# Moving operand read in two alternating halves in the second matmul stage of a fused attention and gated MLP kernel

## The chip, the cores and the metric

The kernel runs on one core of a Trainium2 chip. The metric is the device time of one execution in microseconds (us). Lower is better.

## What is computed

Banded attention with 32 global tokens (8 batches, 8 heads, 512 local tokens, head dimension 64) makes 544 tokens of 512 features per batch. All 4352 tokens then go through a gated MLP without activation:

```python
attn_out = _attn_ref(q_l, k_l, v_l, q_g, k_g, v_g)     # (8, 8, 544, 64)
x = attn_out.transpose(0, 2, 1, 3).reshape(4352, 512)
a = x @ w1                                              # 512 -> 1024
b = x @ w2
h = a * b @ w3                                          # 1024 -> 1024
return h @ w_out                                        # 1024 -> 512
```

All tensors are float32.

## The kernel before

The kernel never forms h. Since nothing stands between w3 and w_out, it first multiplies the two matrices on the chip: `fold` (line 695) makes, for each of 8 blocks t of 128 rows, the 128x512 block t of w3 times w_out in PSUM, in float32. `fold_split` (lines 697 to 702) then splits each block into two tiles of type float32r, `w34h` (the value rounded to float32r, by a copy on ACT or DVE, `hi_of` at line 442) and `w34l` (the rest, by a subtraction on DVE, line 702). There are 8 tiles of each, 128x512, and they stay in SBUF (`W34`).

The tokens are worked on in 17 groups of 256 (two per batch, and one for the 8 x 32 global tokens). For each group there are four quarters, and each does this:

- `first` (lines 548 to 550): x times w1 and x times w2, for two blocks of 128 of the 1024 inner features. A product of two float32 matrices is made of three float32r matmuls (hi by hi, hi by lo, lo by hi); the moving operand is the token tile, 256 columns.
- `gate_a`, `gate_b`, `gate_hi`, `gate_lo`: the product a * b, split into `gh` and `gl` in the same way.
- `second` (lines 568 to 580): for each of the two blocks m and each 128 tokens t, three matmuls into the PSUM tile `acc`, which holds 128 tokens by 512 outputs. The stationary operand is a 128x128 piece of `gh` or `gl`; the moving operand is the whole of `w34h` or `w34l` of block m, 512 columns, read from the first to the last.

After the fourth quarter, `evict` (line 585) copies `acc` to SBUF and `store` writes it to DRAM in rows of 512.

So `second` issues 17 groups x 8 blocks x 2 token halves x 3 = 816 matmuls of 512 columns, and `first` 17 x 8 x 2 x 4 x 3 = 3264 of 256 columns.

The order of the work on each engine is written out by hand: the table `ORDER_OF` (lines 41 to 185) gives every step a place and, with the letters A, D and P, its engine where there is a choice. `add`, `take` and `read` declare what each step depends on, and `in_order` issues the steps by the table. Attention, the folding of the weights and the MLP are interleaved by it. The first matmul of `second` comes at about 108 us in the trace, after all of the folding.

Names used below: `w` is the PSUM tile of the folding, `w3f` and `wo` its operands, `acc` the PSUM tile of `second`, `ap` and `bp` those of `first`, `raw_w`, `raw_wo` and `raw_w12s` weights as they arrive in SBUF, of which each value is a pair of 32-bit words (so that `raw[:, :, 1]`, line 603, reads every other word), `x` the split token tiles, `xr` their source.

Of the kernel before, what the change touches and what calls it, by code (L numbers as in the profile page):

```python
# [14 lines left out]
def f(ap):  # L15
    return ap.bitcast(F32)
# [185 lines left out]
def band_attention_glu_kernel(  # L202
# [14 lines left out]
    nc = tc.nc  # L217
# [57 lines left out]
    T = {}  # L275
# [165 lines left out]
    def hi_of(dst, src, eng=None):  # L441
        (nc.scalar.copy if eng in (None, nc.scalar) else eng.tensor_copy)(dst, src)
# [94 lines left out]
    W12, W34 = {}, {}  # L537
# [30 lines left out]
    def second(key, w, m, ts=None):  # L568
        tw = min(w, 128)
        if m == 0:  # L570
            for t in range(0, w, 128):
                T["acc", key, t] = ps_acc.tile([128, 512], F32, tag="acc", name=f"acc{key[0]}_{key[1]}_{t}")
        wh, wl = W34[m]
        gh, gl = T["gh", m // 2 % 2], T["gl", m // 2 % 2]
        for t in range(0, w, 128) if ts is None else ts:
            sl = slice(t, t + tw)
            a = T["acc", key, t][0:tw]
            nc.tensor.matmul(a, gh[:, m % 2, sl], wh, start=(m == 0), stop=False)  # L578
            nc.tensor.matmul(a, gh[:, m % 2, sl], wl, start=False, stop=False)  # L579
            nc.tensor.matmul(a, gl[:, m % 2, sl], wh, start=False, stop=(m == 7))  # L580
# [116 lines left out]
    def fold_split(t, part, eng=None):  # L697
        if part == 0:
            W34[t] = tuple(const.tile([128, 512], F32R, tag=f"w34{e}{t}", name=f"w34{e}{t}") for e in "hl")
            hi_of(W34[t][0], T["w34", t], eng)  # L700
        else:
            nc.vector.tensor_sub(W34[t][1], T.pop(("w34", t)), f(W34[t][0]))

# [159 lines left out]
    def quarter(k, q):  # L865
# [27 lines left out]
        for ts in parts:  # L893
            for j in range(2):
                me = ("second", k, m + j, ts)
                deps = [("gl", n), ("w34l", m + j)]
                if m + j:
                    deps.append(("second", k, m + j - 1, None if j == 0 or not last else ts))
                if m + j == 0:
                    for e in range(0, w, 128):  # L900
                        take("acc", 2, ("acc", k, e), me)
                add(me, "PE", deps, second, key, w, m + j, ts)
                read(me, ("gh", n), ("gl", n), *[("acc", k, e) for e in range(0, w, 128)])
# [36 lines left out]
    def product(t):  # L940
        take(SUMS[t], 2 if SUMS[t] == "acc" else 1, ("w34", t), ("fold", t, 0))
        for j in range(8):
            add(("fold", t, j), "PE", [("unit", "w3", t, j // 4, 3), ("unit", "wo", j, 0, 3)] + [("fold", t, j - 1)] * (j > 0),
                fold, t, j)
            read(("fold", t, j), ("w34", t), ("w3f", t, j // 4))
        add(("w34h", t), "ACT DVE", [("fold", t, 7)], fold_split, t, 0)
        add(("w34l", t), "DVE", [("w34h", t)], fold_split, t, 1)
        read(("w34h", t), ("w34", t))
        read(("w34l", t), ("w34", t))
# [111 lines left out]
```

## Time and profile before

| | |
|---|---|
| median of the runs | 757.54 us |
| lowest run | 756.35 us |
| profiled execution, first to last instruction (span) | 754.5 us |
| TensorE matmul (PE) busy | 736.1 us, 98% of the span |
| VectorE (DVE) busy | 429.7 us, 57% |
| ScalarE (ACT) busy | 291.6 us, 39% |
| GpSimd (POOL) busy | 115.7 us, 15% |
| mean granted TensorE clock | 0.998 of full speed |

The profile shows the span of the profiled execution. What lies around it isn't in the trace; the median of the runs is 3.0 us above the span. In the profile, PE is the row of matmuls and PEld that of the loads of their stationary operands, which overlap them. The duration of a single matmul holds its way through the array, and the next one starts long before it has ended; so the cost of a matmul in a dense stretch is the distance from its start to the start of the next, its pace, and not its duration.

### The profile page before, as it was taken

To read this page: it belongs to the slowest core of one execution; us is meant where nothing else is said; L and a number is where in the kernel's file an instruction comes from. 1 tells how busy PE (TensorE), PEld (TensorE's weight loads), DVE (VectorE), ACT (ScalarE), POOL (GpSimd) and SP (SyncE) were. 2 spreads that over 40 slices of the span, in tenths; PEclk is the share of its full clock that TensorE was granted. 3 is DMA by queue.
4 is the path that set the end of the run, shared out by engine and by line. 5 is a ranking of instruction groups with operands and counts; after the bars stand their busy time and mean duration, and the time that the engine had idled before them with its cause. 6 is when DMAs were issued, how large, how long until landed. Compare 5 with 4: busy or idle time off the path is not lost.

```text
span 754.5 us, 24083 instructions
## 1 busy us (share of the span) xinstructions
PE 736.1 (98%) x10036; PEld 645.2 (86%) x10036; DVE 429.7 (57%) x1275; ACT 291.6 (39%) x853; POOL 115.7 (15%) x165
## 2 busy tenths in 40 slices
PE   3899999999999999999999999999999999999998
PEld 3355598988999998989999999899998999999997
DVE  2878888675565466555664557655566635432222
ACT  3777886555243333324234323244423242201010
POOL 2043564300020002130120001101020110000000
PEclk9999999999999999999999999999999999999999
DMA  7988578696586665587857396756675955520010
GB/s 238 311 285 252 167 222 244 192 264 165 157 220 168 188 194 153 167 193 197 220 165 202 106 248 189 214 139 174 167 197 168 254 151 135 134 69 15 1 43 29
DMA packets 96500, 131.98 MB, mean 175 GB/s; under 512 B 15592, under 2 KB 57704, under 8 KB 96392
## 3 DMA queue, kind: packets, MB, share of 16 engines
q1 hardware_dynamic: 96392, 130.45, 61.8%
q8 instruction: 79, 1.29, 0.8%
q14 instruction: 29, 0.24, 0.1%
HBM read 92.65 MB, written 37.75 MB: 173 GB/s over the span
## 4 chain that ended last, share of the span: by engine, by line
PE 97%; DMA 2%; SPq 0%; DVE 0%; issue 0%; ACT 0%
PE acc L578 9%; PE ap L548 9%; PE bp L548 9%; PE acc L580 8%; PE acc L579 8%; PE bp L549 8%; PE bp L550 8%; PE ap L549 8%; PE ap L550 8%; PE w L695 8%; PE s L350 4%; PE v L402 4%; PE sg L473 2%; PE gx L502 2%; DMA raw_wo<-in_wo_t_dram 1%; DMA vg<-in_vg_t_dram 1%
## 5 line engine op out<-in xcount | busy, mean ns | idle before, releaser
L548 PE MATMUL ap<-x,w12h 128*128 128x256 f32 x512 | 144.1, 281 | 0.0
L548 PE MATMUL bp<-x,w12h 128*128 128x256 f32 x512 | 144.0, 281 | 0.0
L549 PE MATMUL bp<-x,w12h 128*128 128x256 f32 x512 | 142.1, 277 | 0.0
L550 PE MATMUL bp<-x,w12l 128*128 128x256 f32 x512 | 142.0, 277 | 0.0
L549 PE MATMUL ap<-x,w12h 128*128 128x256 f32 x512 | 142.0, 277 | 0.0
L550 PE MATMUL ap<-x,w12l 128*128 128x256 f32 x512 | 141.9, 277 | 0.0
L362 ACT ACTIVATE P<-P,mn 128x128 f32<-128x128 f32 x256 | 100.4, 394 | 60.8 <-DVE mn L357 29.2
L548 PEld LDWEIGHTS bp<-x,w12h 128*128 128x128 f32 x512 | 96.1, 188 | 4.0 <-issue 1.6
L548 PEld LDWEIGHTS ap<-x,w12h 128*128 128x128 f32 x512 | 96.1, 188 | 3.7 <-issue 1.8
L549 PEld LDWEIGHTS bp<-x,w12h 128*128 128x128 f32 x512 | 96.3, 188 | 2.1 <-issue 0.2
L549 PEld LDWEIGHTS ap<-x,w12h 128*128 128x128 f32 x512 | 96.3, 188 | 1.4
L550 PEld LDWEIGHTS bp<-x,w12l 128*128 128x128 f32 x512 | 96.5, 188 | 0.0
L550 PEld LDWEIGHTS ap<-x,w12l 128*128 128x128 f32 x512 | 96.4, 188 | 0.0
L357 DVE CUSTOM_DVE_ANT_0 P<-s,cs 128x128 f32<-128x128 f32 x256 | 62.5, 281 | 34.9 <-PE s L350 31.4
L695 PE MATMUL w<-wo,w3f 128*128 128x512 f32 x128 | 60.7, 616 | 4.7 <-DVE w3f L609 4.7
L326 POOL COPY K<-K 128x480 f32<-128x480 f32 x24 | 15.8, 662 | 246.5 <-DMA K<-in_kp_t_dram 210.0
L695 PEld LDWEIGHTS w<-wo,w3f 128*128 128x128 f32 x128 | 23.5, 194 | 30.2 <-issue 22.3
L362 ACT ACTIVATION_READ_ACCUMULATOR P<-P,mn 128x1 f32 x256 | 48.3, 189 | 0.0
L316 POOL COPY V<-vg 32x1024 f32<-32x1024 f32 x26 | 27.1, 1049 | 80.7 <-PE gx L507 45.9
L370 DVE STREAM_TRANSPOSE P<-P 128x1024 f32<-128x1024 f32 x28 | 34.7, 1238 | 5.8 <-ACT P L362 5.6
L316 ACT COPY V<-vg 32x1024 f32<-32x1024 f32 x31 | 32.4, 1045 | 14.2 <-PE gx L507 13.5
L350 PE MATMUL s<-K,q 64*32 64x128 f32 x2048 | 37.3, 275 | 0.0
(786 smaller groups left out, 1372.3 us busy)
## 6 DMA issues: line engine op xcount, KB each, us to landing
Pd<-P SPq DMA_DIRECT2D x112, 128.0 KB, 3.0
Pt<-Pd SPq DMA_DIRECT2D x28, 512.0 KB, 4.2
raw_w<-in_w_t_dram SPq DMA_DIRECT2D x24, 512.0 KB, 6.0
V<-in_v_t_dram SPq DMA_DIRECT2D x56, 192.0 KB, 5.3
K<-in_kp_t_dram SPq DMA_DIRECT2D x36, 272.0 KB, 3.9
V<-in_v_t_dram SPq DMA_DIRECT2D x36, 256.0 KB, 5.0
out_dram<-o SPq DMA_DIRECT2D x34, 256.0 KB, 4.0
q<-in_q_t_dram SPq DMA_DIRECT2D x32, 256.0 KB, 4.6
```

The lines of the kernel that those rows point to most:

```text
L316: (nc.scalar.copy if eng is nc.scalar else eng.tensor_copy)(to, src)
L350: nc.tensor.matmul(block(st[:, h], x, 128 * g), q[64 * h : 64 * h + 64, c : c + 32], window(m, h, 4 * g + x), start=True, stop=True, skip_ ...
L357: nc.vector.tensor_tensor_reduce(T["P", m][:, :, h, g], chunks(T["s", m][:, h, 128 * g : 128 * g + 128]), chunks(masks[g]), -0.125, 3.0e38 ...
L362: nc.scalar.activation(P, P, AF.Exp, bias=T["mn", m][:, g, h : h + 1], scale=-1.0, accum_out=T["sm", m][:, g, h : h + 1])
L370: nc.vector.transpose(P, P)
L548: nc.tensor.matmul(d, wh[:, k, c, :], x[:, 0, 0:w], start=(k == m % 2 == 0), stop=False, skip_group_check=True)
L549: nc.tensor.matmul(d, wh[:, k, c, :], x[:, 1, 0:w], start=False, stop=False, skip_group_check=True)
L550: nc.tensor.matmul(d, wl[:, k, c, :], x[:, 0, 0:w], start=False, stop=(k == 3), skip_group_check=True)
L578: nc.tensor.matmul(a, gh[:, m % 2, sl], wh, start=(m == 0), stop=False)
L579: nc.tensor.matmul(a, gh[:, m % 2, sl], wl, start=False, stop=False)
L580: nc.tensor.matmul(a, gl[:, m % 2, sl], wh, start=False, stop=(m == 7))
L695: nc.tensor.matmul(T["w34", t], T["w3f", t, j // 4][:, j % 4], T["wo"][:, j], start=(j == 0), stop=(j == 7))
```

## The change

`fold_split` takes the columns of the product in PSUM in two passes: first the even columns 0, 2, ..., 510, which go to positions 0 to 255 of the tile, then the odd columns, which go to positions 256 to 511. It reads PSUM with a step of two elements (8 bytes) and writes SBUF in one run of 512.

`second` gives the matmul a view of the same tile that runs over the two halves in alternation: position 0, 256, 1, 257, and so on. In this order the columns are 0, 1, 2, 3, ... again, so `acc`, `evict` and `store` are as before. Two columns that follow each other in the stream are 256 elements (1024 bytes) apart in the partition, forward, and then 255 elements back.

```diff
@@ second
-        wh, wl = W34[m]
+        wh, wl = (w.rearrange("p (a c) -> p c a", a=2) for w in W34[m])
@@ fold_split
             W34[t] = tuple(const.tile([128, 512], F32R, tag=f"w34{e}{t}", name=f"w34{e}{t}") for e in "hl")
-            hi_of(W34[t][0], T["w34", t], eng)
+            hi_of(by_halves(W34[t][0]), in_pairs(T["w34", t]), eng)
         else:
-            nc.vector.tensor_sub(W34[t][1], T.pop(("w34", t)), f(W34[t][0]))
+            nc.vector.tensor_sub(by_halves(W34[t][1]), in_pairs(T.pop(("w34", t))), by_halves(f(W34[t][0])))
+
+    def by_halves(ap):
+        return ap.rearrange("p (a c) -> p a c", a=2)
+
+    def in_pairs(ap):
+        return ap.rearrange("p (c a) -> p a c", a=2)
```

No instruction is added, removed or moved: every engine issues the same instructions on the same tiles in the same order, and only the patterns by which the 816 matmuls and the 16 splits address them differ.

## Rows read from the trace of the kernel before

**Rows 1.** The page: span, busy time of each engine, granted TensorE clock.
```profile
span 754.5 us, 24083 instructions
...
PE 736.1 (98%) x10036; PEld 645.2 (86%) x10036; DVE 429.7 (57%) x1275; ACT 291.6 (39%) x853; POOL 115.7 (15%) x165
...
PEclk9999999999999999999999999999999999999999
```

**Rows 2.** Busy time by stretch, with granted clock, DMA share and GB/s last.
```profile
core 0: us, PE busy (x) PEld busy (x) DVE busy (x) ACT busy (x) POOL busy (x), PEclk, DMA share, GB/s
...
107.90:754.50 646.60, 643.13 (x8994) 589.81 (x8992) 350.93 (x1043) 214.06 (x668) 73.91 (x98) 1.00 0.60 163
```

**Rows 3.** All waits of PE: us in total, times, longest.
```profile
PE warm L863 <- POOL og L252: 10.3, 1, 10.3
PE w L695 <- DVE w3f L609: 4.7, 1, 4.7
```

**Rows 4.** The chain that ended last, shares of the span by line.
```profile
by line: PE acc L578 8.8%; PE ap L548 8.8%; PE bp L548 8.6%; PE acc L580 8.3%; PE acc L579 8.3%; PE bp L549 8.3%; PE bp L550 8.3%; PE ap L549 8.3%; PE ap L550 8.3%; PE w L695 7.7%; PE s L350 4.5%; PE v L402 4.3%; PE sg L473 1.8%; PE gx L502
```

**Rows 5.** Timeline of PE around 400 us: start, duration (us), instruction.
```profile
399.35 0.39 PE L580 MATMUL acc<-w34h,gl__5961 128*128 128x512 f32 x1
399.57 0.39 PE L578 MATMUL acc<-w34h,gh__5951 128*128 128x512 f32 x1
399.80 0.39 PE L579 MATMUL acc<-w34l,gh__5951 128*128 128x512 f32 x1
...
400.72 0.39 PE L580 MATMUL acc<-w34h,gl__5961 128*128 128x512 f32 x1
400.95 0.28 PE L548 MATMUL bp<-x,w12h 128*128 128x256 f32 x1
401.06 0.28 PE L549 MATMUL bp<-x,w12h 128*128 128x256 f32 x1
```

**Rows 6.** The page's group of the folding's matmuls: busy us, mean ns | idle before.
```profile
L695 PE MATMUL w<-wo,w3f 128*128 128x512 f32 x128 | 60.7, 616 | 4.7 <-DVE w3f L609 4.7
```

**Rows 7.** The chain from 60 to 82 us, pieces of folding: start, us, what.
```profile
65.70 4.49 PE w L695 x10
...
71.07 1.72 PE w L695 x4
```

**Rows 8.** DVE casts of line 442 by tile: duration ns min/median/max, starts, shapes.
```profile
L442 DVE CAST x<-xr x18: 229/283/294, 155.3 to 639.1; 128x256 fp32r<-128x256 f32 x18
...
L442 DVE CAST w34h<-w x2: 681/686/692, 45.9 to 47.2; 128x512 fp32r<-128x512 f32 x2
L442 DVE CAST w12h<-raw_w12s x2: 294/294/295, 98.0 to 128.5; 128x256 fp32r<-128x256 f32 x2
```

**Rows 9.** Tile w34h: the other splits, and the first matmuls of the second stage.
```profile
L702 DVE TENSOR_TENSOR w34l<-w,w34h x8: 675/684/692, 46.6 to 96.5; 128x512 fp32r<-128x512 f32 x8
L442 ACT CAST w34h<-w x6: 576/586/588, 52.3 to 95.9; 128x512 fp32r<-128x512 f32 x6
...
L578 PE MATMUL acc<-w34h,gh__1203 x4: 388/388/390, 107.9 to 109.9; 128*128 128x512 f32 x4
```

## The prediction

> **What bounds the kernel now.** I read the page first, for which engine is full: PE is busy 736.1 of 754.5 us, at full clock in every slice, while DVE stands at 57% and ACT at 39% [rows 1]. A mean over the span can hide a stage with another limit, so the second view is the busy time from the first matmul of the second stage to the end: PE is busy 643.13 of 646.60 us, at a granted clock of 1.00 [rows 2]. The 3.5 us that are left are the last copy and store. The third view, PE's waits, has two entries, 10.3 us for a cleared tile at the start and 4.7 us for folded weights, both long before 107.9 us [rows 3, 9]. So once the second stage runs, TensorE never waits, and no other engine has to be faster for it. Whatever a matmul of the second stage costs more or less goes into the end time in full, and no cover exists for it.
>
> The chain that ended last says how much of the span these matmuls hold: lines 578, 579 and 580 have 8.8 + 8.3 + 8.3 = 25.4% of 754.5 us, 191.6 us [rows 4]. The code issues 816 of them, so one holds 235 ns of the chain, handovers to other work included. In a dense stretch the timeline gives the pace itself: seven starts from 399.35 to 400.95 us, 1.60 us, 229 ns for 512 columns [rows 5]. The matmuls of 256 columns behind them start 0.11 us apart. The price goes with the columns, as for a stream that is fed one column after the other.
>
> **The change part by part.** The matmuls: none is added, removed or moved, and 816 read their moving operand in another order. Before, four neighbouring float32 columns are 16 bytes in a row; now every column lies 1 KB from the one before. No matmul in this trace reads its moving operand with a step between elements, so the cost has no row and I bound it from both sides.
>
> From below: the folding's matmuls, plain float32, go through the same array with the same tile of 128x512, and the trace has two records for each matmul of the code (128 records, 64 matmuls) [rows 6]. Four records take 1.72 us in a dense stretch, 430 ns each [rows 7]. If such a record stands for two passes over its 512 columns, a pass takes 215 ns, and that is the fastest pace that any stream of 512 columns shows here. The second stage needs 229 ns. Were the new order to free it of the difference, 14 ns x 816 = 11.4 us would go: 743.1 us of span.
>
> From above: the 430 ns record is also the nearest row for a stream that takes each column at half the rate: the same tile shape and element size, two column times per column fetched. And the 14 ns between 215 and 229 say that the float32r stream is already a little slower than the array could go, so what feeds it is close to being the limit. The columns 256 elements apart can no longer come out of one piece of memory that was fetched for its neighbour. If the feeding gave at least two columns per fetch before and gives one now, the pace is at least half: between 430 ns (the record) and 2 x 229 = 458 ns (its own pace doubled). I take the middle, 444 ns, since the first leaves out the 14 ns that this stream now pays and the second doubles them. The term is (444 - 229) x 816 = 175.4 us, with ends of 164.0 and 186.9 us. If each of four columns had come out of one fetch which already sets the pace, it would be 4 x 229 = 916 ns, far above; that end stands among the rivals.
>
> The Trainium skill states a rule that speaks against this change: in "Advanced Engine Details and Errata", section "SBUF Cachelines", SBUF has lines of 16 bytes, at least two hits on a line are needed to absorb the access time, and another line on each access is penalised. It gives no price for TensorE. No run shown so far bears it out or refutes it for a moving operand; by its two-hit limit a pattern with one hit would land at half pace, near the 444 ns above.
>
> The splits: 8 copies and 8 subtractions read PSUM with a step of 8 bytes instead of 4. They take 586 ns on ACT (6), 686 ns on DVE (2) and 684 ns on DVE (8) now [rows 8, 9]. The nearest row for a stepped read is from SBUF: DVE's casts of 128x256 take 294 ns from every other word and 283 ns from a source in runs [rows 8], 11 ns more. I take nothing. Doubled, the sum would be 6 x 0.586 + 2 x 0.686 + 8 x 0.684 = 10.4 us, spread from 46 to 97 us over two engines. That work stands beside PE's folding and attention. Of PE's waits none is for a split [rows 3]; if this cover were gone at every one, all 10.4 us would be on the path. A gain is excluded, since the elements are as many as before.
>
> The rest: gates, evictions, transfers and their order stay. PE's slower pace gives each of them more time between deadlines, and since PE waits for none of them after 107.9 us, that time buys nothing.
>
> The sum: 754.5 + 175.4 + 0 = 929.9 us of span. The median lies 3.0 us above the span of the profiled execution, so 933 us. For the later verdict: a measurement of this kernel can tell about 2%, 15 us, from no change, which is 18.6 ns for each of the 816 matmuls.
>
> **The rivals.** First, the order of the columns costs nothing: what feeds the stream fetches single columns, or runs far enough ahead to hold both lines. For it speaks that stepped reads on DVE cost 11 ns in 283 [rows 8]; against it, that DVE's step of 8 bytes leaves two columns in 16 bytes, and 1 KB leaves one, and that this engine streams fewer columns in the same time (128x256 in 283 ns, 512 in 229 ns on PE). The pace stays 229 ns and the time is 757 us, within 2%. It decides as long as the pace stays under 229 + 18.6 = 248 ns. This is the other side: not slower.
>
> In a sentence beside it: the Trainium skill's page "TensorE: Matmul & The Clock Gate", section "Back-to-back issue gap", gives a pace by the number of columns alone, whatever the pattern of the source, and so has the change at no cost; its own figure of 518 cycles for 512 columns at the full clock is an estimate of 216 ns, which this trace's 229 ns exceeds.
>
> Second, the alternation helps: if the 14 ns come from neighbouring columns colliding in one piece of memory, reading from two places in turn removes them, and the time is 757.5 - 11.4 = 746 us, 1.5% faster. It can't pass 2% unless a pass is faster than any row shows.
>
> Third, the fetch is the limit by more than a factor of two: four columns share one now, and the pace becomes up to 916 ns. The term is (916 - 229) x 816 = 560.6 us, the time 1318 us. Against it, a stream so short of fetches would hardly come within 14 ns of the two-pass record's rate.
>
> Fourth, a part of the cost is hidden by a small buffer ahead of the array: with a pace half way, (229 + 444) / 2 = 336 ns, 87 us more, 845 us.
>
> **How the numbers follow.** Half rate: 0.60, with its own range from 757.5 + 164.0 = 921 to 757.5 + 186.9 = 944, widened by the splits' 10.4 us to 955 and, for less than half rate's full price, down to 890. No cost: 0.20. Partly hidden, 775 to 890: 0.08. Above 955: 0.10. Helped by more than 2%: 0.02. The likeliest case gives 933 us. To leave out no more than 2 in 10, the range must reach to the case of no cost: from 755 to 955 it holds 0.60 + 0.08 + 0.20 = 0.88. Faster 0.02, same 0.20, slower 0.78.
>
> **What would show it.** In the profile after, the starts of L578, L579 and L580 in a dense stretch should stand about 444 ns apart, and those of L548 to L550 0.11 to 0.12 us apart as now; the chain should give the three lines some 40% of the span; PE should be busy all the way behind the first of them; the granted clock should stay at 1.00. The splits should stay at 586 and 684 ns. The prediction is wrong if the starts stay near 229 ns, or if the time comes out longer while they do, by a wait or a lower clock.

## The result and the profile after

The changed kernel takes 744.49 us (median of 4 runs, 744.0 to 746.68) against 756.94 us before (median of 4). One of the four runs before took 1741.61 us, and the ratio, 0.9846 with a 95% interval from 0.9828 to 0.9864, goes by the fast runs alone. The changed kernel is 1.5% faster: clear of no change, but within the 2% that the prediction counted as the same. The prediction was 933 us, slower by nearly a quarter.

The rows of the page that answer to [rows 1], of the changed kernel:

```profile
span 742.2 us, 24082 instructions
...
PE 724.9 (98%) x10036; PEld 645.6 (87%) x10036; DVE 429.2 (58%) x1275; ACT 292.0 (39%) x853; POOL 115.0 (15%) x165
...
PEclk9899999999999999999999999999999999999999
```

The span is 12.3 us shorter than before, and PE is busy 11.2 us less. The other engines work as long as they did. The stretch behind 107.9 us, as in [rows 2]:

```profile
107.90:742.20 634.30, 630.64 (x8991) 589.30 (x8989) 351.36 (x1040) 214.47 (x668) 73.81 (x98) 1.00 0.60 166
```

It is 634.30 us long instead of 646.60, also 12.3 us less. The first matmul of the second stage starts at 107.4 us here, 0.5 us earlier than before, so 11.8 us of the gain lie behind it, where PE is as full as before and the granted clock is 1.00. The waits of PE, as in [rows 3]:

```profile
PE warm L869 <- POOL og L252: 9.0, 1, 9.0
PE w L695 <- DVE w3f L609: 4.7, 1, 4.7
PE v L402 <- DVE raw_w12s L605: 0.2, 1, 0.2
```

The two long ones lie ahead of the second stage, as before, and no wait for a gate, a split or an output tile has come in. The timeline of PE in a dense stretch of the second stage, as in [rows 5] (the rows left out are matmuls of the same three lines):

```profile
401.86 0.38 PE L579 MATMUL acc<-w34l,gh__6050 128*128 128x512 f32 x1
...
403.37 0.38 PE L580 MATMUL acc<-w34h,gl__6097 128*128 128x512 f32 x1
```

From the first row to the second are seven distances, 1.51 us, 216 ns each. Before it was 229 ns. Over the whole trace, the distances from each of the 816 to the next matmul add up to 191.1 us before and 179.8 us now: 11.3 us less, 14 ns each. The rest is the 0.5 us from before the stage and some tenths in the first stage (382.0 to 381.3 us); the spans of thirteen executions of the kernel before differ by more than that, from 752.2 to 757.0 us. The two tiles' splits:

```profile
L702 DVE TENSOR_TENSOR w34l<-w,w34h x8: 676/682/692, 46.4 to 96.1; 128x512 fp32r<-128x512 f32 x8
L442 ACT CAST w34h<-w x6: 586/587/590, 52.1 to 95.4; 128x512 fp32r<-128x512 f32 x6
```

The medians are 682 and 587 ns against 684 and 586 [rows 9]: reading PSUM by every other column costs nothing that these rows show.

### The profile page after: what moved, and what is told of

Its sections match the earlier page's. It is cut to its first block, busy times and chain, and to the rows that moved or that the text cites. A ratio compares the mean times of both kernels' runs of the same rounds, so it can differ in the third digit from the quotient of the medians.

```text
span 742.2 us, 24082 instructions
## 1 busy us (share of the span) xinstructions
PE 724.9 (98%) x10036; PEld 645.6 (87%) x10036; DVE 429.2 (58%) x1275; ACT 292.0 (39%) x853; POOL 115.0 (15%) x165
## 4 chain that ended last, share of the span: by engine, by line
PE 90%; DMA 6%; DVE 1%; POOL 1%; issue 1%; ACT 0%; SPq 0%; DVEq 0%; POOLq 0%
PE ap L548 8%; PE acc L578 8%; PE bp L548 8%; PE ap L549 8%; PE ap L550 8%; PE bp L550 8%; PE bp L549 8%; PE acc L580 8%; PE acc L579 8%; PE w L695 5%; PE v L402 4%; PE s L350 4%; DMA raw_wo<-in_wo_t_dram 3%; PE sg L473 2%; PE gx L502 2%; DMA raw_w12s<-in_w_t_dram 1%
## 5 line engine op out<-in xcount | busy, mean ns | idle before, releaser
L548 PE MATMUL ap<-x,w12h 128*128 128x256 f32 x512 | 143.9, 281 | 0.0
L548 PE MATMUL bp<-x,w12h 128*128 128x256 f32 x512 | 143.8, 281 | 0.0
L549 PE MATMUL ap<-x,w12h 128*128 128x256 f32 x512 | 141.9, 277 | 0.0
L549 PE MATMUL bp<-x,w12h 128*128 128x256 f32 x512 | 141.8, 277 | 0.0
L550 PE MATMUL ap<-x,w12l 128*128 128x256 f32 x512 | 141.8, 277 | 0.0
L550 PE MATMUL bp<-x,w12l 128*128 128x256 f32 x512 | 141.8, 277 | 0.0
L548 PEld LDWEIGHTS bp<-x,w12h 128*128 128x128 f32 x512 | 96.3, 188 | 3.3 <-issue 1.6
L548 PEld LDWEIGHTS ap<-x,w12h 128*128 128x128 f32 x512 | 96.3, 188 | 3.2 <-issue 1.8
L549 PEld LDWEIGHTS bp<-x,w12h 128*128 128x128 f32 x512 | 96.2, 188 | 1.4 <-issue 0.2
L549 PEld LDWEIGHTS ap<-x,w12h 128*128 128x128 f32 x512 | 96.2, 188 | 0.9
L550 PEld LDWEIGHTS bp<-x,w12l 128*128 128x128 f32 x512 | 96.2, 188 | 0.0
L550 PEld LDWEIGHTS ap<-x,w12l 128*128 128x128 f32 x512 | 96.1, 188 | 0.0
```

The lines of the kernel that those rows point to most:

```text
L548: nc.tensor.matmul(d, wh[:, k, c, :], x[:, 0, 0:w], start=(k == m % 2 == 0), stop=False, skip_group_check=True)
L549: nc.tensor.matmul(d, wh[:, k, c, :], x[:, 1, 0:w], start=False, stop=False, skip_group_check=True)
L550: nc.tensor.matmul(d, wl[:, k, c, :], x[:, 0, 0:w], start=False, stop=(k == 3), skip_group_check=True)
```

## The experiments

In all of them the number to read is the distance between starts in the second stage, from two rows of PE's timeline that are seven distances apart; only the moving read of `second` differs from the kernel named, unless something else is said. A time without a ratio beside it is that of one run.

**The order alone.** The splits of the changed kernel, with the read of before:

```diff
-        wh, wl = (w.rearrange("p (a c) -> p c a", a=2) for w in W34[m])
+        wh, wl = W34[m]
```

> The splits write the two halves as in the changed kernel, but the second stage reads the tile in one run of 512; so the 512 output columns come out with the even ones first and the odd ones behind. Theory A (the order of the moving read sets the pace): the starts of L578 to L580 go back to 226 to 232 ns apart, the span to 754.5 us, ratio to before 1.00. Theory B (the splits, or the values' new places in SBUF, bring the gain): the starts stay 216 ns apart and the span near 742 us, ratio 0.985.

```profile
408.56 0.40 PE L579 MATMUL acc<-w34l,gh__6050 128*128 128x512 f32 x1
...
410.18 0.39 PE L580 MATMUL acc<-w34h,gl__6097 128*128 128x512 f32 x1
```

1.62 us / 7 = 231 ns, a span of 755.2 us, and a ratio of 1.0003 (0.9989 to 1.0018). The splits bring nothing and cost nothing. The read's order is the whole effect.

**Three orders that tell why.** On the kernel before:

```diff
-        wh, wl = W34[m]
+        wh, wl = (w.rearrange("p (g a c) -> p g c a", a=2, c=4) for w in W34[m])
```

> The splits are those of before; the second stage reads each group of 8 columns as 0, 4, 1, 5, 2, 6, 3, 7, so that the stream alternates between two neighbouring pieces of 16 bytes; the output columns come out in that order. Theory 1 (two places far apart are needed, the neighbour collides): 226 to 232 ns between starts, span 754 us. Theory 2 (a run of neighbouring columns is what costs, any break of it frees the pace): 216 ns, span 742 us. Theory 3 (one column for each fetch of 16 bytes halves the rate once the fetch can't be kept): 430 ns or more, span 920 us.

```profile
402.93 0.38 PE L579 MATMUL acc<-w34l,gh__6050 128*128 128x512 f32 x1
...
404.44 0.38 PE L580 MATMUL acc<-w34h,gl__6097 128*128 128x512 f32 x1
```

216 ns and 746.46 us, as in the change, with two places only 16 bytes apart: the distance isn't what matters. Theory 1 falls.

```diff
-        wh, wl = W34[m]
+        wh, wl = (w.rearrange("p (c a) -> p a c", a=2) for w in W34[m])
```

> The splits are those of before; the second stage reads columns 0, 2, 4, ..., 510 and then 1, 3, ..., 511, a step of 8 bytes with no alternation; the output columns come out in that order. Theory 1 (two places far apart in turn are needed): 226 ns or more between starts, span 754 us or more. Theory 2 (any break of the run frees the pace): 216 ns, span 742 us. Theory 3 (fetches of 16 bytes): two columns for each fetch, no worse than 229 ns.

```profile
426.90 0.64 PE L579 MATMUL acc<-w34l,gh__5334 128*128 128x512 f32 x1
...
430.08 0.64 PE L580 MATMUL acc<-w34h,gl__5348 128*128 128x512 f32 x1
```

3.18 us / 7 = 454 ns, and 938.39 us in the one run: half rate by a step of 8 bytes, which neither of the two theories left had. Theory 2 falls: a break of the run isn't enough.

```diff
-        wh, wl = W34[m]
+        wh, wl = (w.rearrange("p (c a) -> p a c", a=4) for w in W34[m])
```

> The splits are those of before; the second stage reads columns 0, 4, 8, ..., then 1, 5, 9, ... and so on, a step of 16 bytes with no alternation; the output columns come out in that order. Theory 1 (two places far apart in turn are needed): 226 ns or more between starts, span 754 us or more. Theory 2 (any break of the run frees the pace): 216 ns, span 742 us. Theory 3 (one column for each fetch of 16 bytes halves the rate): 430 ns or more, span 920 us.

```profile
400.67 0.64 PE L579 MATMUL acc<-w34l,gh__4942 128*128 128x512 f32 x1
...
403.90 0.64 PE L580 MATMUL acc<-w34h,gl__4983 128*128 128x512 f32 x1
```

461 ns and 943.55 us. This is the half rate of theory 3 and of the prediction. It exists, with nearly the predicted time, but the change doesn't call it up. And theory 3 alone can't say why a step of 8 bytes, with two columns in each 16 bytes, costs as much as one of 16.

**Two new theories.** P: the memory gives pairs of columns. L: the stream is read in two lanes, of which one takes its even places and the other its odd places. They part where two places are read in turn, with a step of two in each:

```diff
-        wh, wl = W34[m]
+        wh, wl = (w.rearrange("p (a c b) -> p b c a", a=2, b=2) for w in W34[m])
```

> The splits are those of before; the second stage reads 0, 256, 2, 258, ..., 254, 510 and then 1, 257, 3, 259, ...: two places in turn as in the change, but in each place a step of two columns; the output columns come out in that order. Theory P (the memory gives two neighbouring columns, 8 bytes, per fetch, and the fetch is kept for at least one other one; half rate whenever the second column of a pair is not asked for soon): about 450 to 460 ns between starts, span 937 us, as with a step of two alone. Theory L (the stream is read in two lanes, its even and its odd places, and a lane goes at full rate as long as its own step is 8 bytes or less): 216 to 232 ns, span 742 to 755 us.

```profile
408.33 0.40 PE L579 MATMUL acc<-w34l,gh__6050 128*128 128x512 f32 x1
...
409.94 0.39 PE L580 MATMUL acc<-w34h,gl__6097 128*128 128x512 f32 x1
```

1.61 us / 7 = 230 ns, 756.78 us: the run's own time. Under L it has to be so, since a run too gives each lane a step of two columns. P falls, which wanted 450 ns.

The next two change places more often:

```diff
-        wh, wl = W34[m]
+        wh, wl = (w.rearrange("p (a c) -> p c a", a=4) for w in W34[m])
```

> The splits are those of before; the second stage reads 0, 128, 256, 384, 1, 129, ...: four places in turn; the output columns come out in that order. Theory P with room for two fetches only: the second column of a pair comes three fetches later and has to be fetched again, 450 to 460 ns, span 937 us. Theory P with room for four or more: 216 ns, span 742 us. Theory L: each lane jumps by 1 KB at each step, 450 ns or more.

```profile
413.72 0.44 PE L579 MATMUL acc<-w34l,gh__5951 128*128 128x512 f32 x1
...
415.67 0.45 PE L580 MATMUL acc<-w34h,gl__5961 128*128 128x512 f32 x1
```

```diff
-        wh, wl = W34[m]
+        wh, wl = (w.rearrange("p (a c b) -> p c a b", a=2, b=2) for w in W34[m])
```

> The splits are those of before; the second stage reads 0, 1, 256, 257, 2, 3, 258, 259, ...: two places in turn, but a pair of neighbours from each; the output columns come out in that order. If the 10 to 16 ns that the run loses come from one pair following the next out of the same place: 216 ns between starts, span 742 us. If they come from the two columns of one pair being asked for one right behind the other: 226 to 232 ns, span 754.5 us. Theory L: lanes of 0, 256, 2, 258 and 1, 257, 3, 259, at half rate or at full rate as in the run of two places with a step.

```profile
404.13 0.50 PE L579 MATMUL acc<-w34l,gh__5445 128*128 128x512 f32 x1
...
406.41 0.50 PE L580 MATMUL acc<-w34h,gl__5451 128*128 128x512 f32 x1
```

279 ns and 326 ns in these rows, 793.87 and 846.29 us; over all starts in the second stage the medians are 280 and 340 ns. In both orders each lane jumps between two places at every step. L expected half rate for the first and left half rate open for the second, and neither is as bad. That a lane keeps something of the place it left would fit; these runs don't show it.

**How much of a piece a lane uses.** If a lane fetches 16 bytes at a time, the number of its columns in a piece should count, and not its step. An order in which each lane takes two neighbours from each piece:

```diff
-        wh, wl = W34[m]
+        wh, wl = (w.rearrange("p (g a c) -> p g c a", a=2, c=2) for w in W34[m])
```

> The splits are those of before; the second stage reads each four columns as 0, 2, 1, 3; the output columns come out in that order. The stream's even places then ask for columns 0, 1, 4, 5, 8, 9, ..., its odd places for 2, 3, 6, 7, ...: each lane uses two columns of a piece of 16 bytes, neighbours, before it goes on to the next. Theory L16 (each lane fetches 16 bytes at a time, and a fetch that serves two columns falls slightly short of the array): 226 to 232 ns between starts, span 755 us, as the run and as two places with a step. Theory L4 (what a lane needs is a step of one column, whatever the piece): 216 ns, span 742 us.

```profile
407.31 0.40 PE L579 MATMUL acc<-w34l,gh__6050 128*128 128x512 f32 x1
...
408.93 0.39 PE L580 MATMUL acc<-w34h,gl__6097 128*128 128x512 f32 x1
```

231 ns, 756.0 us: theory L16. All orders by what a lane finds in each piece of 16 bytes before it goes on:

| order of the stream | columns per piece and lane | distance |
|---|---|---|
| 0, 256, 1, 257 (the change); 0, 4, 1, 5 | 4 | 216 ns |
| the run; 0, 256, 2, 258; 0, 2, 1, 3 | 2 | 229 to 231 ns |
| 0, 2, 4, 6; 0, 4, 8, 12 | 1 | 454, 461 ns |
| 0, 128, 256, 384, 1; 0, 1, 256, 257, 2 | 4 and 2, but each lane changes pieces at every column | 280, 340 ns (medians of all starts) |

**A rival for the run's loss: the loads.** While a matmul streams, the stationary operand of the next is loaded from SBUF too (PEld is busy 645.2 us beside PE's 736.1 in the 754.5 us of [rows 1]). To see whether the two get in each other's way, the load behind L578 is halved, in the kernel before:

```diff
-            nc.tensor.matmul(a, gh[:, m % 2, sl], wl, start=False, stop=False)
+            nc.tensor.matmul(a[0:64], gh[:, m % 2, t : t + 64], wl, start=False, stop=False)
```

> The kernel before, but the matmuls of line 579 use 64 of 128 columns of the stationary operand, so the hi by lo product is left out for half of the tokens; all moving reads are runs of 512. The load of 64 columns goes on while L578 streams. If the run's loss comes from the load reading SBUF beside it: the distance from L578 to L579 falls from 226 towards 220 ns, and the others stay. If it comes from the moving read alone: it stays at 226 ns, the span at 755 us.

```profile
408.68 0.39 PE L578 MATMUL acc<-w34h,gh__6050 128*128 128x512 f32 x1
408.91 0.39 PE L579 MATMUL acc<-w34l,gh__6050 128*64 128x512 f32 x1
...
409.36 0.39 PE L578 MATMUL acc<-w34h,gh__6050 128*128 128x512 f32 x1
409.59 0.39 PE L579 MATMUL acc<-w34l,gh__6050 128*64 128x512 f32 x1
```

The distance from L578 to L579 is 0.23 us in both pairs, and over all starts in the trace its median is 227 ns, the same as before, though the load for L579 now takes 134 ns instead of 188. The distance from L579 to L580 stays at 229 ns too. The time is 756.84 us. So the loss doesn't depend on the width of the load that goes on beside the read.

**Both stages.** If a run loses, the first stage loses too, with 3264 matmuls. On the changed kernel, the first stage's token tiles are read in alternation, and the stores put the rows in their places:

```diff
@@ first
-            x = X[key[0], k, key[1]]
-            nc.tensor.matmul(d, wh[:, k, c, :], x[:, 0, 0:w], start=(k == m % 2 == 0), stop=False, skip_group_check=True)
...
+            xh, xl = (X[key[0], k, key[1]][:, e, 0:w].rearrange("p (a c) -> p c a", a=2) for e in range(2))
+            nc.tensor.matmul(d, wh[:, k, c, :], xh, start=(k == m % 2 == 0), stop=False, skip_group_check=True)
...
@@ store
-            r = key[0] * S + 32 + 256 * key[1] + t
-            nc.sync.dma_start(out[r : r + 128], o)
+            r = key[0] * S + 32 + 256 * key[1]
+            nc.sync.dma_start(out[r : r + 256].rearrange("(a c) d -> c a d", a=2)[t // 2 : t // 2 + 64], o)
...
+            to = out.rearrange("(a e b s) c -> e b s a c", a=2, e=2, b=2)[t // 128]
+            for x in range(2):
+                nc.sync.dma_start(to[x, 0:32], o[64 * x : 64 * x + 64])
```

> The changed kernel, and the first stage too reads its token tiles in alternation (0, 128, 1, 129, ...), so that the rows of the gate tiles and of the output tiles stand for the tokens in that order; the stores write them to their places. If a run loses in the first stage what it lost in the second (dense starts now 113 to 122 ns apart, the mean of lines 548 to 550 at 116.8 ns): 108 to 110 ns between dense starts, some 5 ns x 3264 = 16 us less than the changed kernel, about 728 us, ratio to before 0.962. If 256 columns are bound by something else, such as the loads of the stationary operand, the starts stay at 113 ns or more: 744 us, ratio 0.984. If the stores by alternating rows delay the output tiles, PE shows waits on o and the time is above 744 us.

Two rows of the first stage in this kernel, fifteen distances apart:

```profile
402.01 0.28 PE L548 MATMUL ap<-x,w12h 128*128 128x256 f32 x1
...
403.69 0.28 PE L548 MATMUL ap<-x,w12h 128*128 128x256 f32 x1
```

1.68 us / 15 = 112 ns. The time is 735.93 us (median), a ratio of 0.9726 (0.9691 to 0.9762) to before: this version beats both kernels. The gain over the changed kernel is about 9 us, not the 16 expected: over all starts in the first stage the median goes from 114 to 112 ns and not to 108 to 110, and the distances add up to 371.7 us instead of 381.3. PE shows no wait on the output tiles.

The same edit on the kernel before, with the second stage in runs:

> The kernel before, with the alternation in the first stage alone (token tiles read as 0, 128, 1, 129, ..., stores to match); the second stage reads in runs. If the gains of the stages are independent: 111 to 112 ns between dense starts in the first stage, 226 to 232 ns in the second, some 9 us less than before, 748 us, ratio 0.988. If the second stage's loss depends on what the first left in place, its starts move from 226 to 232 ns.

```profile
402.73 0.40 PE L579 MATMUL acc<-w34l,gh__6050 128*128 128x512 f32 x1
...
404.34 0.39 PE L580 MATMUL acc<-w34h,gl__6097 128*128 128x512 f32 x1
```

747.93 us, a ratio of 0.9896 (0.9880 to 0.9913), with 230 ns in the second stage. Over all starts one of its distances did move as the second theory had it: from L578 to L579 the median is 234 ns instead of 227, and the 816 add up to 192.4 us instead of 191.1; why is open. The two gains add up within the interval: 0.9846 x 0.9896 = 0.974, and both together measured 0.9726.

Last, what holds the first stage at 112 ns, in the version with both stages:

```diff
-            nc.tensor.matmul(d, wh[:, k, c, :], xl, start=False, stop=False, skip_group_check=True)
+            nc.tensor.matmul(d[0:64], wh[:, k, c, 0:64], xl, start=False, stop=False, skip_group_check=True)
```

> The kernel with both stages in alternation, but the matmuls of line 549 use 64 of 128 columns of the stationary operand, so the hi by lo product of the first stage is left out for half of the inner features. The load of 64 columns goes on while L548 streams. If what keeps the first stage at 111 to 112 ns for 256 columns, against 216 / 2 = 108 ns by the second, is the load of the next stationary operand: the distance from L548 to L549 falls to 108 to 109 ns, the others stay at 111 to 112 ns, the time falls by some 3 ns x 1088 = 3 us. If it is the stream itself or a fixed price of each matmul: all stay at 111 to 112 ns.

```profile
400.01 0.28 PE L548 MATMUL ap<-x,w12h 128*128 128x256 f32 x1
...
401.67 0.28 PE L548 MATMUL ap<-x,w12h 128*128 128x256 f32 x1
```

Fifteen distances take 1.66 us instead of 1.68. Over all starts in the trace, one distance of three falls, by 3 ns from 112 to 109. But it is the distance from L549 to L550, not the expected one from L548 to L549, though the load for L549 takes 138 ns instead of 192. The one run takes 733.86 us, 0.6 us below the lowest of the four with both stages (734.45 to 738.47 us), so the time alone shows no gain. The matmul of half the width is thus followed 3 ns sooner; since it also writes half the output rows, the run doesn't say whether the stationary operand or the output has a part in the 112 ns. A kernel that reads the stationary operands of the first stage in alternation too gave no result, so no run shows what that would do.

## Why the prediction was wrong

- **What bounds the kernel** held. PE was full behind 107.9 us and still is, no other engine gave or took time, and what the matmuls saved went into the end in full: 11.3 us of distances, 12.3 us of span.
- **The splits at nothing** held, by their own rows (682 and 587 ns) and by the run that has them alone (1.0003).
- **The step that failed** is "If the feeding gave at least two columns per fetch before and gives one now, the pace is at least half". The words "gives one now" took the stream for a single reader that forgets a piece as soon as it asks for another. A reader of single columns in turn would have done to the alternation what happened to the steps of two and four. What the runs show in its place is that the even and the odd places of the stream count apart: with the change each of the two keeps to its own half, and finds four columns in a piece of 16 bytes where the run gave it two. Two readers, one for each, are the model for this and no more. The term was put at +175.4 us and measured -11.3 us.
- **The price of half rate** was nearly right and applied to the wrong order: the prediction put it between 430 and 458 ns and took 444, and steps of two and four columns measure 454 and 461 ns, at 938 and 944 us.
- **The lower bound** of 215 ns, from the folding's records read as two passes, was the answer: 216 ns. Whether such a record is two passes, no run shows, so the agreement may hold some luck. The sign was in the prediction's own rows, in the 14 ns between 215 and 229. They were read as a feed close to its limit, which fits the runs, since the order alone moves the pace, and then as a reason that this order must hurt. They were also the most that any order here won.
- **The second rival** named 746 us and got 744.5, and its price (11.4 us) is what the 816 matmuls gave (11.3). Its reason, neighbours that collide in one piece of memory, is only half right: two places 1 KB apart lose as much as the run when each lane uses two columns of a piece (230 ns). It had no share of its own in the chances within 2%, and the case within 2% was told as "no cost". The first rival's bound, a distance under 248 ns, held, but not its cause.
- The 518 cycles for 512 columns of the Trainium skill ("TensorE: Matmul & The Clock Gate", section "Back-to-back issue gap"), which the prediction took for an estimate of 216 ns, agree with the changed kernel's 216 ns; before the change the trace was 13 ns above it. The section calls this the gap of an isolated matmul, which the prediction left out, and gives about 131 ns for 512 columns in a sustained stream of loads and matmuls. The sustained streams here differ: none is faster than 216 ns.

## What to carry to other kernels

When a dense float32r stream's distance between starts lies above what the columns need, look at what the even and the odd places of the moving operand ask for: an order that gives each of them four neighbouring columns, such as two halves in alternation, took 229 ns to 216 ns here, and a median of 114 ns to one of 112 ns in the stage of 256 columns. The data can be laid out for it where it is written anyway, by the splits or the stores. A plain step of two or of four columns costs double here, so a layout that saves a copy by a stepped moving read should be priced at that.

## What the runs showed of the hardware that was not expected

A moving read of float32r in a plain run isn't the fastest one: 229 to 231 ns against 216 ns for 512 columns. A step of 8 bytes halves the rate (454 ns) and one of 16 bytes hardly adds to it (461 ns), while an alternation between two places, 16 bytes or 1 KB apart, each of them read without a step, comes to 216 ns.

Seven of the nine orders fit two lanes, one for the even and one for the odd places of the stream, each of which goes through SBUF in pieces of 16 bytes: four columns per piece come to 216 ns, two fall short of that by 6 to 7%, one halves the rate. That is a model that the distances bear out, and no run looks inside. A rival with one reader, which takes the stream two columns at a time and pays whenever the next two lie in other pieces, gives the same counts (four, two and one) for these seven orders; an order in which the two lanes change pieces at different times might separate them, and no run has one. The two orders in which a lane changes pieces at every column (medians of 280 and 340 ns) show that neither model is complete. The Trainium skill, in "Advanced Engine Details and Errata", section "SBUF Cachelines", asks for two hits on a line of 16 bytes. For the stream as a whole the measurement differs: a step of two has two hits in each 16 bytes and takes 454 ns. Counted by lane it has one, and the sentence agrees so far; but two hits by lane still take 229 to 231 ns where four take 216.
